# Weight chunk loads issued from ScalarE's queue instead of SyncE's, in a fused attention and feed-forward kernel

## The chip, the cores and the metric

The kernel runs on one core of a Trainium2 chip. The metric is the time of one execution on the device, in microseconds. The core has five instruction streams that run side by side and meet only at semaphores: TensorE (PE, with its weight loads shown apart as PEld), VectorE (DVE), ScalarE (ACT), GpSimd (POOL) and SyncE (SP, which here only issues DMAs). A DMA is an instruction in the stream of one of these engines; in the profile such an instruction stands under SPq or ACTq. The bytes are moved by 16 DMA engines that all queues share.

## What is computed

Eight batches of eight attention heads, 576 positions of 64 elements, with a causal mask and a bias from a cumulative sum; the heads' outputs are laid side by side as 4608 tokens of 512 elements, which go through a feed-forward layer of width 2048.

```python
cum = np.cumsum(np.maximum(s, 0.0), axis=-1)
bias = -(cum[:, :, :, None] - cum[:, :, None, :])
scores = q @ k.T / sqrt(64)                       # per head
scores = np.where(causal, -1e9, scores + np.minimum(bias, 0.0))
attn = softmax(scores)
x = (attn @ v), heads side by side                # 4608 x 512
h = x @ w_in                                      # 512 x 2048
g = where(h >= 1, h, where(h <= -1, 0, (h + 1) ** 2 / 4))
y = g @ w_out                                     # 2048 x 512
```

The weights `w_in` and `w_out` are float64 in memory, 8 MB each, and are turned into float32 and then into pairs of float16 on the chip.

## The kernel before

**Weights.** Each of the two matrices is cut into 16 chunks of 128 rows by 512 eight-byte numbers, 512 KB per chunk. The class `Weights` has three steps for a chunk. `load` (L179) takes a raw buffer and issues one DMA from SP's queue (L190). `decode` (L192) turns the raw integers into float32 with an ACT operation (L199), a DVE shift (L200), a PE column sum that gives the scale (L204), and then, on even chunks, an ACT operation (L212) with one DVE operation (L213), on odd chunks two DVE operations (L215, L216). The last of these DVE operations is what frees the raw buffer. `split` (L225) later makes the float16 pair with ACT (L229, L231) and POOL (L232).

The chunks of `w_in` rotate through four raw buffers, so that the load of chunk n waits for the decoding of chunk n-4. The chunks of `w_out` rotate through two buffers of one tag (`raw`) and through buffers of another (`x0`) which they share with the first attention result, so about three of them are in flight. The first three loads of `w_out` also wait, by a small DVE copy into their buffer (L185), for the last scale of `w_in`.

**Attention.** A job is a pair of heads and a half of the query positions; there are 64. `att_load` (L310) fetches q and k of a job from SP's queue (L319, L335) and the rows of the cumulative sum from ACT's queue (L324 to L328, L351, L352). `scores` computes scores on PE (L405 while the first eight jobs run in float32, L410 and L411 after), a masked minimum on DVE (L416), and the exponential on ACT (L427). `weights_t` normalises on POOL, ACT and DVE (L448 to L454) and transposes the result by DMA, from SP's queue (L455). `v` is loaded (L252), split, and transposed too (L381), all from SP's queue. `att_out` multiplies the transposed weights with `v` on PE (L473).

**Feed-forward.** The first half batch is done in float32 on PE (`first_h` L566, `first_y` L584) while the weights are still being decoded and split; all later ones in float16, with three products for each pair (`ffn_h` L534, `ffn_y` L611).

**Order.** The main program first runs four attention jobs beside the decoding of `w_in` (L644 to L654, two weight steps for every four attention slots), then loads the first three chunks of `w_out` (L658), and then runs through the steps of L663, which decode `w_out` in the first eight, compute the float32 half batch, split the weights and end in the steady alternation of attention slots and float16 feed-forward steps. The tile framework orders every engine's stream by priorities and by a timeline that it estimates; an instruction issued on an engine stays at its place in that engine's stream, and a wait in front of it holds what follows on that engine.

**Queues.** SP's stream therefore holds, in one order: the loads of s, q, k, v and of the weights, the store of the cumulative sum (L153) and all DMA transposes. ACT's stream holds its arithmetic, the small loads of the cumulative sum and the stores of the output (L592, L626).

The lines the change touches are L73 and L190.

Of the kernel before, what the change touches and what calls it, by code (L numbers as in the profile page):

```python
# [69 lines left out]
@with_exitstack  # L70
def attention_ffn(ctx: ExitStack, tc: tile.TileContext, qT, kT, vT, s, w_in, w_out, yT):
    nc = tc.nc
    LOADQ, CUMQ = nc.sync, nc.scalar  # L73
    V, A, G, T = nc.vector, nc.scalar, nc.gpsimd, nc.tensor

    cp = ctx.enter_context(tc.tile_pool(name="cp", bufs=1))
# [91 lines left out]
    class Weights:  # L168
# [10 lines left out]
        def load(self, n, after=None):  # L179
            if n < NW:  # L180
                c = self.order[n]
                pool, tag, bufs = self.tags[n % len(self.tags)]
                self.raw[c] = pool.tile([P, NC, 2], I32, tag=tag, bufs=bufs, name=f"{self.name}r{c}")
                if after is not None:
                    V.tensor_copy(self.raw[c][:, 0, :1], after.bitcast(I32))  # L185
                src = self.src(c)
                dst = self.raw[c]
                if len(src.shape) == 4:
                    dst = dst.rearrange("p (j n) t -> p j n t", j=2)
                nc.sync.dma_start(dst, src)  # L190

        def decode(self, n):  # L192
            c, g = self.order[n], n // self.size
# [540 lines left out]
```

## Time and profile before

| | us |
|---|---|
| median of 3 runs | 1121.34 (1119.88 to 1121.64) |
| the profiled execution | 1119.59 |
| span of the profiled execution, first to last instruction | 1117.8 |
| PE busy | 1024.0 |
| DVE busy | 836.8 |
| ACT busy | 731.0 |
| POOL busy | 667.6 |

The page cuts the span into 40 slices and gives the busy share of each engine in tenths. Groups of instructions are named by line, engine and tile. A wait is written as the waiting instruction, an arrow and what came last before it could start. The chain is followed back from the last instruction, at each step to whatever released it. In the timelines the first two numbers of a row are the start and the length in microseconds; the bracket at the end is the idle time of the engine ahead of the row and what ended it.

### The profile page before, as it was taken

The numbers are of one execution on the slowest core, as the hardware profiler recorded it, in microseconds if no ns is written. First come the engines' busy times: TensorE is split into PE (matmuls) and PEld (weight loads), VectorE is DVE, ScalarE is ACT, GpSimd is POOL, SyncE is SP. The second block draws the span as 40 slices with busy tenths as digits, with TensorE's granted clock in tenths as the row PEclk, the third lists the DMA queues.
The fourth block names the chain that finished last, engine by engine and source line by source line (L and its number), as shares of the span: only waits on it lengthen the run. The fifth ranks groups of instructions, "written<-read, shape, count | busy, mean of one in ns | idle before, by whom it ended". The sixth has DMA issues, their size and how long they took to land.

```text
span 1117.8 us, 24800 instructions
## 1 busy us (share of the span) xinstructions
PE 1024.0 (92%) x8366; PEld 787.3 (70%) x8368; DVE 836.8 (75%) x2313; ACT 731.0 (65%) x1703; POOL 667.6 (60%) x1163
## 2 busy tenths in 40 slices
PE   2668897699999999999999999899999999899998
PEld 1335565487777877777778877777778877787787
DVE  7865775778778877878778878777787877887533
ACT  4656669667557774767557774767577765777432
POOL 4642558776557654766557755666557664765522
PEclk9999899699998999999999999999999999999999
DMA  7995633687548763878658763878468763776300
GB/s 237 242 215 144 171 85 90 128 163 157 121 96 186 164 147 75 179 142 174 110 107 184 160 141 77 178 159 165 88 134 188 156 136 78 162 157 140 67 25 19
DMA packets 340774, 154.99 MB, mean 139 GB/s; under 512 B 290856, under 2 KB 322472, under 8 KB 340648
## 3 DMA queue, kind: packets, MB, share of 16 engines
q1 hardware_dynamic: 330944, 143.49, 60.3%
q10 hardware_dynamic: 9704, 9.93, 2.9%
q8 instruction: 66, 1.08, 0.4%
q14 instruction: 60, 0.49, 0.1%
HBM read 72.31 MB, written 9.73 MB: 73 GB/s over the span
## 4 chain that ended last, share of the span: by engine, by line
PE 55%; DVE 14%; POOL 9%; DMA 8%; ACT 7%; issue 6%; ACTq 0%; SPq 0%; DVEq 0%; POOLq 0%
PE h L534 23%; PE y L611 22%; PE px L473 3%; DMA pt<-pb 3%; PE s L410 3%; DVE pb L454 3%; PE s L411 3%; DMA wor<-in_moe_w_out_dram 2%; POOL pb L448 2%; POOL pb L451 2%; DVE p L416 2%; ACT p L427 2%; ACT u L546 2%; DVE Q L355 1%; DVE h L549 1%
## 5 line engine op out<-in xcount | busy, mean ns | idle before, releaser
L611 PE MATMUL y<-g,WT 128*128 128x256 f16 (+1 forms) x2880 | 427.5, 287 | 8.9 <-POOL g L599 6.9
L534 PE MATMUL h<-x,WT 128*128 128x256 f16 (+1 forms) x2880 | 428.6, 287 | 2.8 <-DVE x L491 2.1
L611 PEld LDWEIGHTS <-WT 128*128 128x128 f16 x2880 | 269.1, 98 | 84.1 <-issue 13.9
L534 PEld LDWEIGHTS <-WT 128*128 128x128 f16 x2880 | 270.6, 98 | 78.4 <-issue 6.0
L427 ACT ACTIVATE p<-p,mn 64x64 f32<-64x64 f32 (+4 forms) x320 | 179.2, 560 | 143.2 <-DVE mn L416 121.7
L599 POOL TENSOR_TENSOR g<-u,g 128x256 f16<-128x256 f32 (+1 forms) x240 | 189.6, 790 | 134.0 <-ACT g L598 133.1
L448 POOL TENSOR_SCALAR pb<-p,rs 64x128 f16<-64x128 f32 (+4 forms) x160 | 97.5, 610 | 213.6 <-DVE rs L444 140.7
L546 ACT ACTIVATE u<-h,ub,us 128x256 f32<-128x256 f32 (+1 forms) x240 | 139.4, 581 | 123.7 <-PE h L534 114.9
L549 DVE SCALAR_TENSOR_TENSOR h<-h,ws,u 128x256 f32<-128x256 f32 (+1 forms) x240 | 123.8, 516 | 102.3 <-ACT u L546 99.8
L451 POOL TENSOR_TENSOR pb<-p,pb 64x128 f16<-64x128 f32 (+4 forms) x160 | 172.8, 1080 | 9.5
L454 DVE SCALAR_TENSOR_TENSOR pb<-p,rs,pb 64x128 f16<-64x128 f32 (+4 forms) x160 | 139.0, 869 | 48.0 <-POOL pb L448 47.9
L416 DVE CUSTOM_DVE_ANT_0 p<-s,mask 64x64 f32<-64x64 f32 (+4 forms) x320 | 134.8, 421 | 32.7 <-PE s L411 22.0
L410 PE MATMUL s<-K,Q 128*64 128x64 f32 (+1 forms) x336 | 126.9, 379 | 17.4 <-DVE mn L416 10.3
L550 DVE SCALAR_TENSOR_TENSOR u<-u,r,h 128x256 f32<-128x256 f32 (+1 forms) x240 | 121.8, 507 | 6.6 <-DVE h L549 0.5
L449 ACT ACTIVATE p<-p,rs 64x64 f32<-64x64 f32 (+4 forms) x160 | 89.6, 560 | 55.4 <-DVE rs L444 53.7
L411 PE MATMUL s<-K,Q 68*64 68x64 f32 (+1 forms) x336 | 103.8, 310 | 4.4 <-DMA K<-cumd 3.2
L598 ACT CAST g<-u 128x256 f16<-128x256 f32 (+1 forms) x240 | 100.7, 419 | 5.9 <-DVE u L550 5.9
L450 POOL TENSOR_SCALAR pb<-p 64x128 f16<-64x128 f32 (+4 forms) x160 | 91.4, 571 | 15.2 <-ACT p L449 14.0
L473 PEld LDWEIGHTS <-vt 128*64 128x64 f16 x1536 | 72.8, 114 | 37.7 <-issue 21.5
L473 PE MATMUL px<-pt,vt 128*64 128x256 f16 (+3 forms) x1536 | 83.6, 260 | 10.7 <-DMA pt<-pb 7.8
L410 PEld LDWEIGHTS s<-K,Q 128*64 128x64 f32 (+1 forms) x336 | 62.1, 185 | 28.6 <-DVE mn L416 9.6
L411 PEld LDWEIGHTS s<-K,Q 68*64 68x64 f32 (+1 forms) x336 | 62.7, 187 | 7.7 <-ACT x L490 3.1
(115 smaller groups left out, 1139.3 us busy)
## 6 DMA issues: line engine op xcount, KB each, us to landing
rk<-in_k_dram SPq DMA_DIRECT2D x56, 288.0 KB
v<-in_v_dram SPq DMA_DIRECT2D x32, 288.0 KB
rq<-in_q_dram SPq DMA_DIRECT2D x56, 160.0 KB
rk<-in_k_dram SPq DMA_DIRECT2D x56, 160.0 KB
wir<-in_moe_w_in_dram SPq DMA_DIRECT2D x16, 512.0 KB
wor<-in_moe_w_out_dram SPq DMA_DIRECT2D x16, 512.0 KB
rq<-in_q_dram SPq DMA_DIRECT2D x56, 128.0 KB
out_dram<-o ACTq DMA_DIRECT2D x32, 160.0 KB
```

The source lines that it names most:

```text
L410: T.matmul(sc[:R, :c1 - c0], Q1[:, hd, qo:qo + R], K1[:, hd, c0:c1], start=True, stop=False)
L411: T.matmul(sc[:R, :c1 - c0], Q2[:KC, hd, qo:qo + R], K2[:KC, hd, c0:c1], start=False, stop=True)
L416: ttr[0] = V.tensor_tensor_reduce(out=Pt[:R, c0:c1], in0=sc[:R, :c1 - c0], in1=mask[:R, mo:mo + c1 - c0], scale=-0.125 if j < F32_JOBS els ...
L427: A.activation(Pt[:R, :W], Pt[:R, :W], AF.Exp, bias=m2[:R], scale=-1.0, accum_out=sums[n, i][:R, hd:hd + 1])
L451: G.tensor_tensor(los[1], pw, his[1], ALU.subtract)
L454: V.scalar_tensor_tensor(los[0], pv, rs[:R, :1], his[0], ALU.mult, ALU.subtract)
L473: T.matmul(px[hd * D:(hd + 1) * D, lo:N], VT[:, vl * NB + j, hd * D:(hd + 1) * D], PT[:, 4 * j + 2 * hd + pl, lo:], start=(m == 0), stop=( ...
L534: T.matmul(h[:, :N], w1.out[ft // 4 * NKT + kt][:, wl, ft % 4 * P:(ft % 4 + 1) * P], x[:, kt, xl], start=(n == 0), stop=(n == 3 * NKT - 1),)
L546: first = A.activation(u, h[:, :N], AF.Relu, bias=ubi[b], scale=usc[b][:, fg:fg + 1]).ins
L549: V.scalar_tensor_tensor(h[:, :N], h[:, :N], wsc[b][:, fg:fg + 1], u, ALU.mult, ALU.max)
L599: G.tensor_tensor(g[:, 1], u, g[:, 0], ALU.subtract)
L611: T.matmul(ys[b, hf, m][:, :N], w2.out[8 * (m // 2) + ft // 2][:, wl, c0:c0 + P], g[:, gl], start=(ft == 0 and n == 0), stop=(ft == NFT - ...
```

## The change

All 32 loads of weight chunks are issued from ACT's queue. Nothing else in the source is different: the same transfers into the same buffers with the same dependencies.

```diff
@@ -70,7 +70,7 @@
-    LOADQ, CUMQ = nc.sync, nc.scalar
+    LOADQ, CUMQ, WQ = nc.sync, nc.scalar, nc.scalar
@@ -187,7 +187,7 @@
                 if len(src.shape) == 4:
                     dst = dst.rearrange("p (j n) t -> p j n t", j=2)
-                nc.sync.dma_start(dst, src)
+                WQ.dma_start(dst, src)
```

Because the framework orders the streams by an estimated timeline, the places of other instructions in their streams can differ too.

## Prediction

> **What bounds the kernel now.** I read the page first, then the busy time by stage, then the chain and ACT's waits inside the stage that holds the weight loads.
>
> ```profile
> span 1117.8 us, 24800 instructions
> PE 1024.0 (92%) x8366; PEld 787.3 (70%) x8368; DVE 836.8 (75%) x2313; ACT 731.0 (65%) x1703; POOL 667.6 (60%) x1163
> PE   2668897699999999999999999899999999899998
> q1 hardware_dynamic: 330944, 143.49, 60.3%
> q10 hardware_dynamic: 9704, 9.93, 2.9%
> ```
>
> PE is the bound from about the eighth slice on; before that it idles. The queue rows show how lopsided the issue is: q1, which carries SP's DMAs, has 143.49 MB, q10, with ACT's, 9.93 MB. The 32 chunks of 512 KB (16.8 MB) would move from the first to the second. The busy time by stage:
>
> ```profile
> 0.00:226.00 226.00, 161.26 (x715) 102.25 (x718) 158.19 (x431) 147.00 (x291) 132.40 (x208) 0.92 0.66 164
> 226.00:650.00 424.00, 410.26 (x3647) 326.12 (x3647) 337.29 (x948) 290.61 (x709) 267.74 (x487) 0.99 0.69 144
> 650.00:1080.00 430.00, 418.80 (x3699) 328.98 (x3698) 328.76 (x909) 281.82 (x678) 258.76 (x457) 1.00 0.62 131
> ```
>
> The columns are the stage, its length, busy PE, PEld, DVE, ACT, POOL, the granted clock, the DMA share and GB/s. The first 226 us leave PE idle for 226.0 - 161.3 = 64.7 us; the two steady stages leave 13.7 and 11.2 us. The loads are all issued before 143 us, so whatever the change does directly it does inside those 64.7 us. Which part of them hangs on the loads is read from ACT's waits and from the chain:
>
> ```profile
> ACT WT L199 <- DMA wor<-in_moe_w_out_dram: 21.1, 11, 5.3
> ACT WT L199 <- DMA wir<-in_moe_w_in_dram: 13.3, 7, 4.0
> ```
>
> ```profile
> 27.36 6.05 DMA wir<-in_moe_w_in_dram
> 37.88 4.76 DMA wir<-in_moe_w_in_dram
> 77.45 6.59 DMA pt<-pb
> 84.08 1.65 PE px L473 x18
> 95.86 7.98 DMA wor<-in_moe_w_out_dram
> 116.44 4.11 DMA wor<-in_moe_w_out_dram
> 126.71 6.09 DMA wor<-in_moe_w_out_dram
> 142.62 4.05 DMA wor<-in_moe_w_out_dram
> ```
>
> ACT stands 21.1 + 13.3 = 34.4 us for weight chunks that have not landed, and the chain goes through six of their transfers, 33.0 us of it. Most of such a transfer is flight, which another queue does not shorten; what the change can take away is the time that a load stands in SP's stream after its buffer is free.
>
> **Part 1: loads no longer stand behind SP's transposes.** From the timelines of SP, DVE and ACT I match each load with the DVE operation that frees its buffer. In `w_in` chunk n waits for chunk n-4.
>
> ```profile
> 27.36 0.46 SPq L190 DMA_DIRECT2D wir<-in_moe_w_in_dram  x1
> 35.04 2.67 SPq L381 DMA_TRANSPOSE vt<-vb  x1
> 37.88 0.93 SPq L190 DMA_DIRECT2D wir<-in_moe_w_in_dram  x2
> 139.47 3.04 SPq L455 DMA_TRANSPOSE pt<-pb  x1
> 142.62 0.52 SPq L190 DMA_DIRECT2D wor<-in_moe_w_out_dram  x1
> ```
>
> ```profile
> 25.03 0.68 DVE L213 SCALAR_TENSOR_TENSOR WT<-wir,WT 128x512 int32<-128x512 int32 x1
> 35.81 0.68 DVE L216 SCALAR_TENSOR_TENSOR WT<-wir,WT 128x512 int32<-128x512 int32 x1
> 36.61 0.69 DVE L213 SCALAR_TENSOR_TENSOR WT<-wir,WT 128x512 int32<-128x512 int32 x1
> 140.18 0.68 DVE L213 SCALAR_TENSOR_TENSOR WT<-wor,WT 128x512 int32<-128x512 int32 x1
> ```
>
> ```profile
> 33.44 0.66 ACT L199 ACTIVATE WT<-wir 128x512 f32<-128x512 f32 x1 [2.75 <-DMA wir<-in_moe_w_in_dram]
> 42.66 0.66 ACT L199 ACTIVATE WT<-wir 128x512 f32<-128x512 f32 x1 [1.26 <-DMA wir<-in_moe_w_in_dram]
> 44.38 0.67 ACT L199 ACTIVATE WT<-wir 128x512 f32<-128x512 f32 x1 [1.06 <-DMA wir<-in_moe_w_in_dram]
> 146.69 0.68 ACT L199 ACTIVATE WT<-wor 128x512 f32<-128x512 f32 x1 [5.34 <-DMA wor<-in_moe_w_out_dram]
> ```
>
> Chunk 8's buffer is free at 25.03 + 0.68 = 25.71 and its load starts at 27.36: 1.65 late, and ACT then waits 2.75 for it. Chunks 11 and 12 have buffers at 36.49 and 37.30, and SP, held in a transpose issue until 37.71, issues them at 37.88 and about 38.35: 1.39 and 1.05 late, with ACT's waits 1.26 and 1.06. A gain can be no more than the smaller of lateness and wait: 1.65 + 1.26 + 1.05 = 3.96 us. In `w_out` the last chunk's buffer is free at 140.86 and the load starts at 142.62, behind a transpose issue of 3.04 us: 1.76 late, against a wait of 5.34, on the chain. Together **5.7 us**. The last two loads of `w_in` are later still by this reading, but the chain between 44 and 74 us runs through PE, DVE and POOL and touches no load, so I count nothing for them. Against all of it: the load must stand in ACT's stream where ACT arrives in time. Bounds 0 to 5.7.
>
> **Part 2: transposes no longer stand behind weights.** The transpose at 77.45 takes 6.59 us on the chain, with three `w_out` chunks issued on the same queue since 72.70. The nearest undisturbed row is
>
> ```profile
> 205.04 4.19 DMA pt<-pb
> ```
>
> so it could come 2.4 us sooner, and PE begins px at 84.08 on its arrival. But what the transpose gains by sharing the 16 engines, the chunks lose. Bounds 0 to 2.4; I take the middle, rounded down, **1.1 us**, since both rows lie on the chain.
>
> [...]
>
> **Part 3: what ACT pays to issue.** The loads by their rows:
>
> ```profile
> L190 SPq DMA_DIRECT2D wir<-in_moe_w_in_dram x16: 327/431/603, 1.4 to 56.5; - x16
> L190 SPq DMA_DIRECT2D wor<-in_moe_w_out_dram x16: 368/398/519, 72.7 to 142.6; - x16
> ```
>
> 16 x 0.431 + 16 x 0.398 = 13.3 us of ACT's stream. ACT is busy 147.0 of the first 226 us, 65%, so some 8.6 us of it would fall on work. How much of that reaches the end depends on ACT's share of the chain. Where the weights are split after the last load, ACT carries most:
>
> ```profile
> by line: POOL WT L232 13.2%; ACT WT L229 9.3%; issue 8.2%; ACT WT L231 7.3%; POOL pb L451 6.9%; POOL pb L448 5.8%; DVE pb L454 5.3%; DMA pt<-pb 4.9%; DMA wor<-in_moe_w_out_dram 4.7%; ACT p L427 4.6%; POOL K L358 4.4%; DMA vt<-vb 4.0%; POOL
> ```
>
> That is 9.3 + 7.3 + 4.6 = 21% of the chain from 140 to 226 us. I take a fifth: **1.7 us** lost, between 0 (ACT's 34.4 us of waits cover it) and 8.6.
>
> **Part 4: the small loads share the queue.** The cumulative sum's rows, until now alone on ACT's queue, would stand behind chunks. Only the first job has no lead: its exponential starts straight after them.
>
> ```profile
> 16.34 0.35 ACT L427 ACTIVATE p<-p,mn 64x64 f32<-64x64 f32 x1 [7.74 <-DMA KF<-ch]
> 0.00:30.00 30.00, 9.27 (x21) 3.73 (x21) 21.51 (x53) 13.14 (x24) 15.45 (x32) 1.00 0.80 235
> ```
>
> At the 235 GB/s of the first 30 us a chunk takes 2.2 us. One or two may be ahead, but SP's first q, k and v no longer wait behind three of them, which works the other way. Between -2.2 and 4.4; I take half a chunk, **1.1 us** lost.
>
> **Part 5: ACT held at a load until DVE frees the buffer.** This is the added wait; behind it in ACT's stream are the exponentials and decodes that DVE, POOL and PE wait for. Where ACT would be waiting for a chunk anyway it costs nothing, which is the case I forecast; the other end is a rival below.
>
> The sum is -5.7 - 1.1 + 1.7 + 1.1 = **-4.0 us**. The profiled execution took 1119.59, 1.75 below the median, and a shift of 4.0 holds for either: 1115.6 from the one, **1117.3** from the median 1121.34, which is the forecast, 0.36% faster. About 0.2%, 2.2 us, is what a measurement of this kernel can tell from no change.
>
> **Rival A: no change (0.27).** For it: the loads are mostly flight, and in the fifth and sixth slices, 112 to 168 us, PE is already busy eight and nine tenths, so a chunk that lands sooner there ends little sooner. If part 1 gives only one chunk, 1.7, and part 2 nothing, parts 3 and 4 take it back: 1122.4; with nothing on either side 1121.3. Against it: the chain does go through the loads. [...]
>
> **Rival B: slower, ACT held at loads (0.24).** The place is the middle of `w_out`.
>
> ```profile
> 105.04 2.57 ACT L212 ACTIVATE wor<-wor,floor_bias 128x512 uint16<-128x512 uint8 x2
> 109.64 0.99 DVE L213 SCALAR_TENSOR_TENSOR WT<-wor,WT 128x512 int32<-128x512 int32 x1
> 115.03 1.34 DVE L213 SCALAR_TENSOR_TENSOR WT<-wor,WT 128x512 int32<-128x512 int32 x1
> ```
>
> ACT is done with chunks 6 and 8 at 107.6 at the latest, and DVE frees their buffers at 110.6 and 116.4, 3.0 and 8.8 us later. ACT now works on in that time. If the loads stand directly behind the decode in ACT's stream, ACT is held for up to 11.8 us here; PE, DVE and POOL run dry behind it. With three quarters of that, 8.9, and the forecast's gain of 4.0 kept, the time is 1126.2; without the gain 1130.2. It decides once ACT is held for more than about 6 us in all. Against it: the framework places a load where it estimates the buffer to be free.
>
> **Rival C: another order (0.07).** The moved loads shift the estimated timeline, and the order after 226 us changes too. PE idles 24.9 us in those two stages; a tenth to a fifth more, with part 1 lost to it, is 2.5 to 5 us: 1124 to 1126.
>
> **The chances.** The forecast, a gain over 2.2 us, has 0.42, rival A 0.27, B and C together 0.31. The range goes from parts 1 and 2 at their upper ends with nothing paid and part 4 at its better end, -5.7 - 2.4 - 2.2 = -10.3, so 1111, to rival B without the gain, 1130. The forecast's own range is 1111 to 1119.
>
> **What would show it.** Right: the loads of chunks 8, 11 and 12 within half a microsecond of the DVE operation that frees them, ACT's 34.4 us of waits for chunks down to under 30, the transpose after the first `w_out` loads under 5 us, and a first stage that is shorter by 4 us with steady stages unchanged. Wrong: waits of ACT at L190 for L213 or L216 of several us, the first exponential later than 18 us, or a difference that sits after 226 us.

## The result, and the profile after

The changed kernel takes **1131.98 us** (median of 4 runs, 1130.29 to 1134.89) against 1121.32 us of the kernel before on the same chip: the ratio is 1.0101, with a 95% interval of 1.0084 to 1.0118. It is 10.7 us slower, where 4 us faster was forecast, and lies outside the range of 1111 to 1130. The profiled execution took 1130.41 us.

The page of the changed kernel, the rows that answer to those of before:

```profile
span 1128.6 us, 24783 instructions
PE   2467998599999999999999999989999999899998
q1 hardware_dynamic: 324288, 126.71, 54.9%
q10 hardware_dynamic: 16360, 26.71, 7.9%
```

The 16.8 MB of weights went from q1 to q10, as the change says. PE's second and fourth slices (28 to 56 and 85 to 113 us) have a four and a seven where before had a six and an eight. The busy time by stage of the changed kernel, with the columns as before (length, PE, PEld, DVE, ACT, POOL, clock, DMA share, GB/s), first in two parts up to 226 us and then the steady stages:

```profile
0.00:100.00 100.00, 46.98 (x159) 24.30 (x160) 69.15 (x202) 48.88 (x102) 47.98 (x96) 0.97 0.92 222
100.00:226.00 126.00, 109.85 (x491) 74.97 (x491) 86.56 (x219) 93.46 (x179) 78.14 (x101) 0.85 0.47 111
226.00:650.00 424.00, 410.00 (x3640) 325.53 (x3640) 339.27 (x948) 288.58 (x704) 269.94 (x491) 0.99 0.69 144
650.00:1080.00 430.00, 415.94 (x3683) 325.94 (x3683) 330.23 (x913) 284.20 (x681) 259.33 (x459) 1.00 0.63 132
```

The same two parts of the kernel before:

```profile
0.00:100.00 100.00, 57.85 (x198) 31.92 (x200) 73.32 (x219) 53.83 (x113) 49.70 (x100) 0.97 0.84 220
100.00:226.00 126.00, 103.41 (x518) 70.33 (x518) 84.87 (x212) 93.17 (x179) 82.70 (x109) 0.88 0.53 120
```

By 100 us PE has done 10.9 us less than before (46.98 against 57.85). From there to 226 us it is busy 87% of the time, against 82% before, and makes up 6.4 us of busy time, so that 4.4 us are still missing at 226 us. Most of PE's delay thus arises in the first 100 us. The granted clock does not explain it: over the first 280 us it is 0.92 in this profile, 0.93 in before's, and 0.89 in that of a kernel below (e4) which is faster than both.

A mark that all kernels of this study share is the first output row at L625, which closes the startup. The groups of that line in the window from 200 to 420 us, first before and then after (count, shortest, median and longest in ns, then the start of the first and of the last):

```profile
L625 ACT ACTIVATE o<-y,ys x12: 460/472/527, 271.9 to 401.7; 128x256 f32<-128x256 f32 x8, 128x320 f32<-128x320 f32 x4
```

```profile
L625 ACT ACTIVATE o<-y,ys x12: 455/470/527, 279.1 to 409.2; 128x256 f32<-128x256 f32 x8, 128x320 f32<-128x320 f32 x4
```

The startup of the changed kernel ends 7.2 us later. The rest, from there to the end of the span, took 849.5 us against 845.9; over all profiles of this study it lies between 844 and 854 us whatever the order or the queue, and two profiles of one and the same kernel (e4, below) have 845.9 and 849.6 us. Those 3.6 us of the 10.8 between the two profiles are therefore left unexplained. A profile shows a single execution, so differences of a few microseconds between two profiles, here and below, are not more certain than this.

The surprise is what became earlier. ACT's waits for chunks in the changed kernel:

```profile
ACT WT L199 <- DMA wor<-in_moe_w_out_dram: 17.5, 10, 5.7
ACT WT L199 <- DMA wir<-in_moe_w_in_dram: 10.9, 5, 5.7
```

They fell from 34.4 to 28.4 us, and the last decode of `w_out` in ACT's timeline starts at

```profile
138.87 0.67 ACT L199 ACTIVATE WT<-wor 128x512 f32<-128x512 f32 x1 [1.82 <-DMA wor<-in_moe_w_out_dram]
```

that is 7.8 us earlier than before (146.69). (The decode of a chunk begins with this ACT operation; the last decode is that of the last chunk.) But behind that decode there is more left to do. The busy time from the last decode to the first L625, before and then after:

```profile
146.69:271.90 125.21, 107.88 (x781) 82.99 (x780) 91.85 (x248) 95.54 (x211) 94.25 (x145) 0.90 0.56 119
```

```profile
138.87:279.10 140.23, 123.81 (x845) 94.16 (x846) 101.88 (x263) 102.84 (x225) 98.71 (x152) 0.89 0.52 115
```

15.9 us more of PE's busy time is left (123.81 against 107.88), and the stretch is 15.0 us longer: -7.8 + 15.0 = +7.2. The attention, on the other hand, came later. On PE a job ends with px, the product of its attention weights with `v` (L473). The third px of PE's timeline, before and then after:

```profile
73.05 1.65 PE L473 MATMUL px<-pt,vt 128*64 128x320 f16 x18 [1.10 <-DVE r_wi L223]
```

```profile
84.88 1.65 PE L473 MATMUL px<-pt,vt 128*64 128x320 f16 x18 [1.17 <-DMA pt<-pb]
```

**The `w_out` weights came sooner and the attention later.** The streams of the two kernels differ in the startup only (up to 243 us), and there they differ on every engine: moving 32 loads between two queues made the framework's estimated timeline another one, and with it the order.

### The profile page after: what moved, and what is told of

Read it like the earlier page. It is cut to its first block, busy times and chain, and to the rows that moved or that the text cites. A ratio compares the mean times of both kernels' runs of the same rounds, so it can differ in the third digit from the quotient of the medians.

```text
span 1128.6 us, 24783 instructions
## 1 busy us (share of the span) xinstructions
PE 1027.3 (91%) x8368; PEld 789.8 (70%) x8368; DVE 841.7 (75%) x2313; ACT 732.0 (65%) x1703; POOL 666.9 (59%) x1163
## 4 chain that ended last, share of the span: by engine, by line
PE 58%; DVE 14%; DMA 9%; POOL 7%; issue 7%; ACT 4%; ACTq 0%; SPq 0%; DVEq 0%; POOLq 0%
PE h L534 22%; PE y L611 21%; DMA pt<-pb 3%; PE px L473 3%; PE s L410 3%; DMA wor<-in_moe_w_out_dram 3%; DVE pb L454 3%; PE s L411 3%; PE y L584 2%; PE h L566 2%; DVE p L416 2%; POOL pb L448 2%; DVE Q L355 2%; ACT u L546 2%; DVE h L549 1%
## 5 line engine op out<-in xcount | busy, mean ns | idle before, releaser
L611 PEld LDWEIGHTS <-WT 128*128 128x128 f16 x2880 | 269.6, 98 | 82.1 <-issue 12.1
L410 PE MATMUL s<-K,Q 128*64 128x64 f32 (+1 forms) x336 | 127.5, 380 | 20.5 <-DVE mn L416 10.8
L473 PEld LDWEIGHTS <-vt 128*64 128x64 f16 x1536 | 74.0, 114 | 48.4 <-issue 35.2
L473 PE MATMUL px<-pt,vt 128*64 128x256 f16 (+3 forms) x1536 | 83.7, 261 | 17.1 <-DMA pt<-pb 11.9
```

The lines of the kernel that those rows point to most:

```text
L410: T.matmul(sc[:R, :c1 - c0], Q1[:, hd, qo:qo + R], K1[:, hd, c0:c1], start=True, stop=False)
L473: T.matmul(px[hd * D:(hd + 1) * D, lo:N], VT[:, vl * NB + j, hd * D:(hd + 1) * D], PT[:, 4 * j + 2 * hd + pl, lo:], start=(m == 0), stop=( ...
L611: T.matmul(ys[b, hf, m][:, :N], w2.out[8 * (m // 2) + ft // 2][:, wl, c0:c0 + P], g[:, gl], start=(ft == 0 and n == 0), stop=(ft == NFT - ...
```

## The experiments

The expectations call theories by letters. **S**: two loaded queues share the DMA engines, above all in the `w_in` part. **S'**, refined: `w_in` loads that SP had held behind the attention's transposes, those of chunks 14 and 15 above all, are let go early and get in the transposes' way. **S2**: any later `w_in` load on a second queue slows the transposes beside it. **O**: the order costs, not the queue. **H**: ACT is held at loads. The flight of a DMA is the time from its issue to its landing. All results are ratios to the kernel before on the same chip, with the 95% interval in brackets; 0.001 is 1.1 us.

**Which loads.** Four kernels issue a part of the loads from ACT's queue (`WQ`), with the condition in L190; the framework makes its own order for each.

```diff
-                WQ.dma_start(dst, src)
+                (WQ if self.name == "wi" else nc.sync).dma_start(dst, src)            # e1
+                (WQ if self.name == "wo" else nc.sync).dma_start(dst, src)            # e2
+                (WQ if self.name == "wi" and n < 4 else nc.sync).dma_start(dst, src)  # e3
+                (nc.sync if self.name == "wi" and n < 4 else WQ).dma_start(dst, src)  # e4
```

> Only the 16 chunks of w_in are issued from ACT; w_out's stay on SP. Theory S (two loaded queues share the DMA engines while the DMA engines are already full, which is in the w_in stage, and ACT waits for the later chunk with attention behind it): most of the 10.7 us is here, +6 to +11. Theory H (ACT held at loads in the middle of w_out, rival B): 0 to +2. Theory O (another order): no firm number.

> Only the 16 chunks of w_out are issued from ACT; w_in's stay on SP. Theory S: -2 to +3, since the DMA engines have room there. Theory H: +7 to +11. Theory O: no firm number.

> Only the first four chunks of w_in, which need no freed buffer, are issued from ACT. If the first microseconds are what costs (s, q and v beside four chunks at once; the cumulative sum is ready later): +2 to +5. If the cost comes from the later stretch around 40 to 54 us: -1 to +1.

> The first four chunks of w_in stay on SP, the other 28 are issued from ACT. Theory S: +5 to +10, little less than the whole change. If the first microseconds are what costs: +2 to +6.

Measured: e1 1.0116 (1.0075 to 1.0157), e2 1.0069 (1.0046 to 1.0091), e3 1.0001 (0.9985 to 1.0017), e4 0.9980 (0.9962 to 0.9997). In microseconds that is +13.0, +7.7, +0.1 and -2.2. These parts do not add up. The first four loads cost nothing, the other 28 win 2 us, and all 32 together lose 10.7. An issue cost or a wait of ACT could be expected to add up; an order that is made anew for each kernel need not. S missed with e2 and e4, and e4, with 28 of the 32 loads on ACT's queue, is faster than before, so that queue as such is not what loses. e2's 7.7 us lie where H had them, but ACT is not held there: no wait at L190 (count, shortest, median, longest in ns) is longer than 17 ns.

```profile
L190 ACTq EVENT_SEMAPHORE  x12: 17/17/17, 73.4 to 141.4; - x12
```

**Order and queue apart.** The next kernels let the framework make its order with one assignment of queues, and then build the program with another, chaining every instruction of an engine to its predecessor in that order; only the loads are left out of the chains. The core of it:

```diff
+    order = build(..., queue_ref)[1]
+    nc = build(..., queue_run, order)[0]
...
+            for k in order:
+                i = traced[k]
+                if i.name in loads: continue
+                if i.engine in last: tc.add_manual_dep(i, last[i.engine].name, NoSync, reason="order")
+                last[i.engine] = i
```

> Every engine's order of instructions is pinned to that of the kernel before, the 32 loads aside, which are issued from ACT at places that the framework picks. Theory O (the other order of the startup costs the time): -4 to +2 against before. Theory S (the second loaded queue and its sharing of the DMA engines): +6 to +11. Theory H (ACT held at loads): +4 to +11.

> Every engine's order is pinned to that of the changed kernel, the 32 loads aside, which are issued from SP as before, at places that the framework picks. Theory O: +8 to +13 against before. Theory S and theory H: -1 to +3.

> The order of e4 (first four w_in loads on SP, other 28 on ScalarE) kept on every engine, but all loads issued from SP. If e4 is 2 us under before because of its order, and its transposes of 10 us beside loads cost it something (S2): the pairs take 5 to 7 us, time -2 to -7 us. If e4's order lives on loads that pass SP's transposes: slower than e4, by 5 us or more.

> The kernel of e4 (first four w_in loads on SP, other 28 on ScalarE, the scheduler's own order) once more, on this chip: -4 to 0 us if its first result holds.

| order of | loads on SP's queue | loads on ACT's queue (e4: 28 of the 32) |
|---|---|---|
| before | 1 by definition | x1: 1.0082 (1.0053 to 1.0110) |
| after | x2: 1.0095 (1.0068 to 1.0121) | after: 1.0101 (1.0084 to 1.0118) |
| e4 | x11: 1.0046 (1.0029 to 1.0064) | e4: 0.9980 (0.9962 to 0.9997), again 0.9961 (0.9942 to 0.9979) |

**After's order is slow on either queue**: with all loads back on SP the kernel still loses 10.7 us. In after's order the queue changes nothing that can be measured, in before's order ACT's queue costs 9 us, and in e4's order it wins 7.4 or 9.5 (x11 against e4's two results). So x2 came out as O had it, while x1, at +9, lies outside O's range and within those of S and H; x11 is over 5 us slower than e4, as its second forecast said. An order thus fits the queue that it was made for in two cases of three, and after's order is a bad one for both.

H does not hold for x1 either: the longest wait of ACT at a load is 0.394 us.

```profile
L190 ACTq EVENT_SEMAPHORE  x16: 17/17/394, 14.7 to 138.2; - x16
```

How one order can lose on both queues shows at the first px. PE's timeline of before, of after, and of x2 there:

```profile
48.34 1.65 PE L473 MATMUL px<-pt,vt 128*64 128x320 f16 x18
60.31 1.65 PE L473 MATMUL px<-pt,vt 128*64 128x320 f16 x18
```

```profile
48.37 0.59 PE L204 MATMUL sum_wi<-WT,ones 128*128 128x512 bf16 x1 [3.89 <-DVE WT L200]
53.74 1.65 PE L473 MATMUL px<-pt,vt 128*64 128x320 f16 x18 [4.79 <-DMA pt<-pb]
```

```profile
53.16 0.58 PE L204 MATMUL sum_wi<-WT,ones 128*128 128x512 bf16 x1 [6.80 <-DVE WT L200]
53.67 1.65 PE L473 MATMUL px<-pt,vt 128*64 128x320 f16 x18
```

Before's first two jobs start at 48.34 and 60.31; after and x2 are over 5 us late with the first. With the loads on ACT's queue the chunk's column sum that the order puts ahead of px is done at 49, and px waits 4.79 us for the transpose. With the loads on SP the transpose is there, but PE, in its order, waits 6.80 us for that column sum, whose chunk SP issued late (4.87 us after its buffer was free). In these two profiles two different waits end within 0.1 us of each other. The lateness grows from there: the third px starts at 84.88 and 85.71, against 71.9 to 76.1 in the profiles of before's order whose `w_in` loads are on SP (before, x4, x6, x13).

The accounting of the last decode holds for all of them. From the last decode of `w_out` to the first L625 the eleven profiles in before's order (before, x1, x3 to x7, x9, x10, x12, x13) have between 124.6 and 125.5 us; after and x2 have both 140.2; e4, its repeat and x11 139.5 to 139.7. Within one order, the startup ends as late as the last decode comes, plus a constant of that order. The constant says how late the startup ends, not why the decode comes when it does. The last decode of e4, and then of x11:

```profile
128.49 0.66 ACT L199 ACTIVATE WT<-wor 128x512 f32<-128x512 f32 x1
```

```profile
135.42 0.65 ACT L199 ACTIVATE WT<-wor 128x512 f32<-128x512 f32 x1
```

e4's order leaves as long a stretch behind the last decode as after's, but brings the decode to 128.5, 18.2 us before before's: -18.2 + 14.3 = -3.9, and its L625 is at 268.0. On SP's queue the same order gets the decode at 135.4 only, and the gain is gone.

**What the queue costs in before's order.** x1 still loses 9 us though no instruction but the loads has moved in any engine's stream. And it does so though ACT waits for chunks 10.2 us less than before, 24.2 against 34.4:

```profile
ACT WT L199 <- DMA wor<-in_moe_w_out_dram: 15.6, 8, 5.5
ACT WT L199 <- DMA wir<-in_moe_w_in_dram: 8.6, 8, 2.1
```

In its chain of waits the first pair of transposes issued together (job 0's last, job 1's first) stands as

```profile
43.82 10.59 DMA pt<-pb
```

and px follows at 54.45; before had issued the pair at 43.39 and begun px at 48.34. S' put this down to chunks 14 and 15.

> Before's order on every engine, loads from ScalarE's queue, but ScalarE issues the w_in loads of chunks 14 and 15 only after its first instruction at L484 (job 0's part of the attention is then past its transposes). Theory S' (the last two w_in loads, let go early, fly beside the pair of attention transposes and make it late): the pair lands as early as before, first px at 48 to 51 us (before 48.3, the same order with these loads not held 54.5), time -1 to +5 us. Rival, two queues as such or ScalarE held at loads: first px near 54, +7 to +10 us.

> Before's order and all loads on SP; only the load of w_in chunk 14 is moved on SP to stand directly behind chunk 13's, ahead of the first attention transposes. Theory S': one early load suffices for a part of the loss: first px 51 to 54 us, +2 to +6 us. Rivals that put the loss on ScalarE's queue or on ScalarE: first px 48 to 49, within 1.5 us of before.

> Before's order on every engine, only the w_in loads from ScalarE's queue, w_out's on SP. Theory S' (the loss lies at the end of the w_in part): first px 53 to 55 us, +5 to +9 us. Rival, ScalarE held in the w_out part: first px 48 to 50, 0 to +2 us.

> Before's order on every engine, w_in loads on SP, only w_out's from ScalarE's queue. Theory S': first px 48 to 50 us, 0 to +3 us. Rival, ScalarE held in the w_out part: +5 to +10 us with first px unchanged.

x3 adds a chain from the loads of chunks 14 and 15 to the first instruction of L484, x4 moves one load within SP's order, x5 and x6 change `queue_run` to `w_in` or `w_out` alone on ACT. Measured: x3 1.0108 (1.0073 to 1.0143), x4 1.0003 (0.9987 to 1.0019), x5 1.0052 (1.0030 to 1.0075), x6 1.0027 (1.0008 to 1.0047). **S' fell.** In x3 the first px did come back, to 51.78, but not the time, which at +12.1 us is the largest loss in before's order; PE's timeline of x3:

```profile
51.78 1.65 PE L473 MATMUL px<-pt,vt 128*64 128x320 f16 x18
67.50 1.65 PE L473 MATMUL px<-pt,vt 128*64 128x320 f16 x18
```

The held loads left at 54.57 and 55.09, beside the next transpose (issued at 54.85), which takes 8.33 us on x3's chain, and the chain goes on from it to the second px: 67.50 against 60.31 before. x4 moved a load the other way, early on SP, and the time did not change. x4's first px, 52.32, is where S' had it, but so is x6's, where S' had it at 48 to 50:

```profile
52.34 1.65 PE L473 MATMUL px<-pt,vt 128*64 128x320 f16 x18 [0.65 <-DMA pt<-pb]
```

Up to there x6 has before's order and before's queue, so from one execution (or chip) to another the first px moves by 4 us without any cause that is tested here. Of the profiles in before's order only x1's 54.45 and x5's 57.48 lie outside of that. In time, x5's +5.9 us is where S' had it, and x6's +3.1 at the edge. In x5 another transpose was hit; its chain:

```profile
34.65 15.05 DMA vt<-vb
```

15 us for a transpose that took 5.6 in before (issued 35.04, used at 40.65). That led to S2: not two loads but any load on the other queue.

> Before's order, w_in loads of the first nine chunks (issued by about 30 us) from ScalarE's queue, all others on SP. Theory S2 (what costs is the later w_in loads flying on a second queue beside the attention's transposes): no transpose pair takes over 7 us, first px 48 to 52 us, time -2 to +2 us. Rival F (what costs is the first four loads beside the cum and v loads at the very start): +5 to +9 us.

> The complement: before's order, w_in loads of the first nine chunks and all of w_out on SP, those of the last seven w_in chunks from ScalarE's queue. Theory S2: some transpose of the startup takes 9 to 15 us, time +4 to +9 us. Rival F: no more than +1 us.

x9 and x10 split the `w_in` loads of x5 at chunk 9 (`n < 9`, `n >= 9`). x9 1.0007 (0.9992 to 1.0022) as S2 had it, which clears the first four loads and whatever they do to the loads of q, k and v; x10 1.0021 (1.0006 to 1.0037), slower but only 2.4 us, under the 4 that S2 expected at least; no transpose of x10's startup took more than 7.8 us, where S2 had 9 to 15.

> Before's order, w_in loads from ScalarE's queue as in x5, but each load is two DMAs whose rows are cut into pieces of 1 KB (4 KB before). [...]

In x7 each `w_in` load is two DMAs that go through the rows in pieces of 1 KB. The DMA view from 20 to 60 us (queue, packets, MB, share of 16 engines), x5 and then x7:

```profile
q10 hardware_dynamic: 1479, 5.29, 51.7%
```

```profile
q10 hardware_dynamic: 6020, 5.80, 52.7%
```

The packets of q10 have 3.6 KB on average in x5 and 1.0 KB in x7. The question is whether the pieces' size makes the transposes beside the loads late, and with them the kernel. x7 takes 1.0066 (1.0047 to 1.0084), no less than x5. Its slowest transpose takes 8.0 us (issued 37.75), far from x5's 15.05, but the time is +7.4 us, against x5's +5.9. So with small pieces the long flight was not there in this one profile, and the loss was. ACT's issue time rose from 6.3 to 14.0 us with the doubled loads, and that too cost nothing that can be told apart. How a load and a transpose that fly together share the engines is not shown by these runs.

> Before's order and queues; added are two loads of 512 KB that nothing reads (w_in chunks 14 and 15 into buffers that w_out uses later), issued by ScalarE behind its pass over w_in chunk 11, at about 43 us, when SP issues job 0's last transpose. Theory S2 (weights on a second queue slow the transposes that fly beside them): first px at 52 to 56 us (before 48 to 52), and 3 us or more later than with the same two loads on SP; time +2 to +6 us. Rival, the bytes alone count: first px and time as with the loads on SP.

> As the run with two extra loads on ScalarE's queue, but SP issues them, directly behind job 0's last transpose. S2: that transpose is not touched, first px 48 to 52 us; the next transposes stand behind 1 MB, some 3 to 4 us; time 0 to +4 us, below the run with ScalarE's queue by 2 us or more. Rival, the bytes alone count: the same time in both.

The last two add 1 MB of loads that nothing reads, near the first pair, to the kernel before: from ACT (x12, at 44.5 and 47.6) or from SP (x13, at 44.6 and 45.3).

```diff
+                if c == 11:
+                    for x in (14, 15):
+                        raw = ap.tile([P, NC, 2], I32, tag="raw", bufs=2, name=f"extra{x}")
+                        nc.scalar.dma_start(raw, w1.src(x))    # x12; nc.sync in x13
```

PE's first px in x12, and then in x13 (the line is L477 there):

```profile
52.38 1.65 PE L477 MATMUL px<-pt,vt 128*64 128x320 f16 x18 [2.07 <-DMA pt<-pb]
```

```profile
48.23 1.65 PE L477 MATMUL px<-pt,vt 128*64 128x320 f16 x18
```

px waits 2.07 us for its transpose in x12 and not at all in x13. That is not enough to show S2: in x4 and x6, with no load on ACT's queue at that time, it waits 1.54 and 0.65 us and starts at 52.3 as well. The time is 1.0008 (0.9987 to 1.0028) for x12 and 1.0019 (1.0002 to 1.0037) for x13, the same for both within the intervals, where S2 had x12 slower by 2 us or more. So S2 failed its own test on time, and its slowed transpose does not stand out here from what executions differ by.

**What is settled and what is not.** Settled: a loss as large as that of the changed kernel is there with its order alone (x2), and no wait of ACT at a load is needed for it. Shown beside it: in an order made for SP's queue, ACT's queue alone costs 9 us (x1). Either is enough, and together they cost no more than one of them. Which of the two acts in the changed kernel these runs cannot say; at its first px it is a late transpose that PE waits for, in x2 a late chunk. Not settled either is through which flights the queue costs time. In before's order the halves add up: `w_in` and `w_out` alone give 0.0052 + 0.0027 = 0.0079 of x1's 0.0082. First nine, last seven and `w_out` give 0.0007 + 0.0021 + 0.0027 = 0.0055; with their intervals this agrees too, so the cost may be spread over the whole startup, but no single place was found that holds it.

**The better version.** e4 beats both kernels: 0.9980 and 0.9961 of before, some 2 to 4 us less. Its source differs from after's in the queue of four loads, and its order is another again. Its order alone, with all loads on SP, is slower than before (x11); its 28 loads on ACT's queue in before's order were not run.

## Why the prediction was wrong

**Part 1, the loads, was right at ACT and wrong at the end; it is the step that failed.** The forecast took 5.7 us from ACT's waits. They fell by 6.0 (34.4 to 28.4), and the loads leave as their buffers come free: those of chunks 8, 11 and 12, which the forecast named, 0.03, 0.95 and 0.10 us behind the DVE operation. For chunks 9 and 10, DVE's and then ACT's timeline of after:

```profile
31.92 0.67 DVE L216 SCALAR_TENSOR_TENSOR WT<-wir,WT 128x512 int32<-128x512 int32 x1
33.31 0.68 DVE L213 SCALAR_TENSOR_TENSOR WT<-wir,WT 128x512 int32<-128x512 int32 x1
```

```profile
32.62 0.38 ACTq L190 DMA_DIRECT2D wir<-in_moe_w_in_dram  x1
34.02 0.36 ACTq L190 DMA_DIRECT2D wir<-in_moe_w_in_dram  x1
```

0.03 us behind the operation that frees them, both. The step that failed is the next one: it equated a wait taken off ACT with time at the end, and took for granted that the order around the loads stays. The order did not stay: decodes moved ahead of attention, a last decode that is 7.8 us earlier left 15.0 us more behind it, and in place of a gain of 5.7 us the startup as a whole ended 7.2 us later. Nor does the equation hold where the order stays: in x1 ACT's waits for chunks fell by 10.2 us and the time rose by 9. And x2 and after, with one order, differ by 9.9 us in these waits (38.3 and 28.4) and by nothing that can be measured in time.

**Part 2, transposes, brought no gain.** It took -1.1, with an upper end of -2.4, from the transpose behind the first `w_out` loads (6.59 us in before). In before's order with `w_out` on ACT's queue the same transpose takes 6.44 us (x1's chain) and 7.22 (x6's). Earlier, with all `w_in` loads on a second queue, the slowest transpose of the first 72 us took, from its issue to the last of its completion events in the trace, 10.6 us in x1, 9.0 in x3, 15.0 in x5 and 12.2 in after; with all `w_in` loads on SP it took 6.9 in before and at most 8.4 elsewhere (x11). Yet e4, which is faster, has one of 8.9, and what these flights cost at the end was not found. After the first `w_out` loads, where under 5 us was to be seen, SP's timeline of after has

```profile
71.68 9.10 SPq L455 DMA_TRANSPOSE pt<-pb  x2
```

a pair whose issue alone takes 9.10 us. In these runs, with two loaded queues, no gain like that upper end is seen. Nor did the two queues move more together: between 20 and 60 us q1 and q10 took 90.2% and 0.6% of the 16 engines' time in before, at 223 GB/s, and 50.1% and 49.0% in after, at 207. And the flight of the loads did not get shorter on the other queue: from the issue to the end of the last packet, by the packet records of the two traces, the median is 4.7 us in before and 5.1 in after for `w_in`, and 3.9 and 4.1 for `w_out`. On after's chain one `w_in` chunk is in flight for 11.34 us, where the longest `w_in` flight on before's chain was 6.05.

```profile
41.98 11.34 DMA wir<-in_moe_w_in_dram
```

**Part 3, ACT's issue cost, +1.7**, cannot be told apart in after. e4 pays for 28 of the 32 issues, 10.5 us of ACT's stream, and is faster all the same; x7 pays 7.7 us more than x5 and is slower by no more than the intervals allow.

**Part 4, the small loads.** The first exponential starts at 17.65, 1.31 us later than before; 1.1 was forecast, and 18 was the point from which it would have been wrong. x9, where it starts at 17.74, shows what that is worth at the end: nothing that can be measured.

**Part 5 and rival B.** The group of L190's semaphores in after (count, shortest, median, longest in ns):

```profile
L190 ACTq EVENT_SEMAPHORE  x19: 17/17/2350, 16.6 to 133.2; - x19
```

The longest hold of ACT at a load is 2.35 us, far from the 11.8 of the rival. B forecast the sign and nearly the size (1130.2), by a mechanism that did not happen.

**Rival C, another order (0.07), named one of the two causes that were shown**, at the wrong place and too small: it looked for it after 226 us and for 1124 to 1126. The orders differ in the startup only, and with the loads on SP's queue after's order costs 10.7 us (x2). That a framework which estimates a timeline may move everything near a moved load was known from the code, and deserved more than 0.07. Rival A, no change, does not describe this case either: in an unchanged order the other queue costs 0.8% (x1). That second cause, the queue itself, stood in no rival.

**The last two loads of `w_in`**, for which I counted nothing, were one of the suspects. In x4 the load of chunk 14 leaves at 45.06 instead of 52.78, and the time is 1.0003: this bears the zero out for that one.

## What to carry to other kernels

Where a framework orders the streams by an estimated timeline, moving an instruction to another queue is two changes, a queue and an order; build the new order on the old queue and the old order on the new queue before giving either the blame. A wait that shrinks on an engine that feeds the bound is not yet a gain: x1 took 10 us of such waits away and lost 9. Look at how much of the bound's work is left behind the last such step. And loads on a second queue were not free of the first: in x5 a transpose that flew beside them from the other queue took 15.05 us, where before had 5.6. Before a difference of a few microseconds inside two profiles is given a cause, look how far profiles of the same order lie apart at that place.

## What the runs showed that was not expected

The constant of an order: from the last decode to the first output, eleven profiles with the same order and last decodes between 144.7 and 156.3 us agree within 0.9 us. Cutting the weights' pieces from 4 KB to 1 KB did not slow that queue: it moved 5.80 MB in 40 us, against 5.29. And 1 MB of loads that nothing needs, in the busiest part of the startup, cost about 2 us or less (1.0019 on SP's queue, 1.0008 on ACT's; by the intervals no more than 4). The first px of one and the same order moved by 4 us between executions (48.2 to 52.3).
